# A fused Fourier mixing and shrink block: the activation's steps spread evenly over three quarters of a pass, the fourth transform step behind a product's copy, and a third PSUM bank for the transforms

## The chip, the cores and the metric

The kernel runs on one core of a Trainium2 chip, in 32-bit floating point throughout. The metric is the device time of one execution in microseconds (us); where several runs were made, their median. TensorE (PE) multiplies matrices into PSUM, which has eight banks of 2 KB for each of 128 partitions; ScalarE (ACT), VectorE (DVE) and GpSimd (POOL) do the rest, and SyncE (SP) issues most transfers. Each engine carries out its own queue in order, and semaphores tie the queues together.

## The reference

The first half mixes each sequence by a filter in the frequency domain, the second is an up projection, a shrink and a down projection:

```python
# x: (8, 3008, 256); filters: (1505, 256); w_in: (256, 2048); w_out: (2048, 256)
X = np.fft.rfft(x, axis=1)
Y = X * (filt_r + 1j * filt_i)[None]
y = np.fft.irfft(Y, n=3008, axis=1)
h = y.reshape(24064, 256) @ w_in
out = (h - np.tanh(h)) @ w_out
```

## The kernel before

**Transforms.** 3008 = 64 x 47, so a Fourier transform is cut into small matmuls. The eight batches are taken in five groups: batch 0, pairs (1,2), (3,4), (5,6), and batch 7. For each group there are four kinds of step. `first` (L351) multiplies input rows into the PSUM tile `pf`, and ScalarE copies it out. `middle` multiplies into `pz` (L430); ScalarE makes two half copies `zs` of it (L443 and L444), VectorE multiplies `pz` by the filter's real part (L445, which the program orders behind those copies), and GpSimd multiplies `zs` by the imaginary part (L446) and adds (L447), giving `uv`. `back`, one step later, multiplies `uv` into `pe` (L411), which ScalarE copies out (L414). `last` multiplies into `pu` (L511), which ScalarE copies into `ut` (L513), and GpSimd forms the four combinations `tu` (L524 to L527, a helper shared with the shrink).

**Passes.** The two projections run over 48 column groups, each of 512 tokens (fewer in the last group of a batch or pair). A group is taken in four passes (the loop variable U, 192 in all), each for a quarter of the 2048 hidden features. Both projections use a 2 x 2 Strassen-like scheme of seven products in place of eight, on halves of 256 tokens. So "product 4" is the fourth of seven, and each product is two matmuls of 128x128 by 128x256. Pass U does, interleaved: the up projection of pass U, the shrink of pass U-1, and the down projection of pass U-2. Function `up` writes this order out by hand, and calls `s()`, `d()` and `e()` for the next step of the shrink, of the down projection and of its tail, and `t(k)` for at most one transform step at "quarter" k.

**Up projection.** Seven products (all at L545) go to three PSUM banks, X, Y and Z, in the order X1, Y2, X6, Z5, X7, X4, Z3: a product adds onto what the bank holds. Copies on ScalarE (L551) keep X's state after products 1, 6 and 7 as `s1`, `u2` and `u3`; VectorE then writes the four blocks of h: Y + s1 (L569), Z + u3 (L583), X itself (L590) and Z + u2 (L596). The next product into X has to wait for the copy of X: product 7 for u2, product 4 for u3, product 1 of the next pass for L590.

**Shrink.** h - tanh(h) is approximated for small |h| by h * y * ((A y + B)^2 + K), where y is the square of arctan(S h). It works on two halves of h, called 2 (blocks 2 and 3) and 0 (blocks 0 and 1), each 128 x 1024. For each: Arctan (L611) and Square (L612, which also leaves row sums that a later check of the range reads) and a second Square (L618), all on ScalarE; a product with h (L617) and a fused add and multiply (L621) on VectorE. The text calls L617 of half 0 mul(0), and L621 of half 0 L621(0). When both halves are done GpSimd forms the combinations t for the down projection (L524 to L527).

**Down projection.** At L663, into four banks o0 to o3 that gather over the four passes of a group: products 1 and 2, then 3 and 5, then 6 and 7, then 4. In the second pass of the group after (those with U = 1 modulo 4) a tail works the sums off: L676 and L682 on ScalarE, L677, L683, L688, L689 and L695 on VectorE, L690 and L696 on GpSimd. The output's transposes (L713, VectorE) come in the pass after that, at quarter 2.

**Order in a pass on TensorE.** X1, Y2, t(0), down 1 and 2, t(1), X6, Z5, down 3 and 5, t(2), X7, down 6 and 7, t(3), X4, down 4, t(4), Z3. Which quarters hold a transform step is laid down by positions computed per batch group; in passes with U = 3 modulo 4, quarters 0 and 2 hold the two `last` steps. The eighth PSUM bank, T, and the bank of Y are what transforms use: function `zd` gives T, or at quarters 1 to 3, if the transform before had T, Y's bank. Asking for a tile in a bank makes its first writer wait for the last reader of the tile before it.

**Stages.** From about 160 to 480 us nearly every quarter holds a transform step (the dense stage); then come, for each pair of batches, a stage with `first` steps and one with `middle` and `back` steps (the latter two from 710 to 1150 us and, for the next pair, some 570 us later); then the same with the single last batch; from about 2455 us on no transforms.

Of the kernel before, what the change touches and what calls it, by code (L numbers as in the profile page):

```python
# [9 lines left out]
F32 = mybir.dt.float32  # L10
# [133 lines left out]
def kernel(  # L144
# [10 lines left out]
    V, G, ACT = nc.vector, nc.gpsimd, nc.scalar  # L155
# [367 lines left out]
    def combine(b, t, shared=False):  # L523
        G.tensor_sub(t[0], b[0][1], b[0][0])  # L524
        G.tensor_sub(t[1], b[1][1], t[0])  # L525
        (V if shared else G).tensor_sub(t[2], b[1][1], b[0][1])  # L526
        G.tensor_sub(t[3], t[1], b[1][0])  # L527
# [4 lines left out]
    def up(U, d, e, s, t):  # L532

        i, u = divmod(U, 4)
        b, tu, w = uts[i]
        rhs = [b[0][0], b[1][0], b[1][1], tu[:, 3, 0:w], tu[:, 0, 0:w], tu[:, 1, 0:w],
               tu[:, 2, 0:w]]
        banks = {k: ps.tile([128, 2, 256], F32, tag=k, bufs=1, name=k) for k in "xyz"}
        X, Y, Z = (banks[k][:, :, 0:w] for k in "xyz")
        h = dn.tile([128, 4, 2, 256], F32, tag="h", bufs=3, name="h")  # L540
        hs[U] = (h, w)

        def mm(bank, q, first):
            for k in range(2):
                nc.tensor.matmul(bank[:, k], wu[:, q - 1, (2 * u + k) * 128:(2 * u + k + 1) * 128],  # L545
                                 rhs[q - 1], start=(first and k == 0), stop=True,
                                 skip_group_check=True)

        def copied(tag):
            t = dn.tile([128, 2, 256], F32, tag=tag, bufs=1, name=tag)[:, :, 0:w]  # L550
            ACT.copy(t, X)  # L551
            return t

        steps_at = ([1, 2, 0, 1, 0, 1, 1, 0] if U > 1 else [0, 0, 1, 0, 2, 0, 1, 2])

        def shrinks(at):
            for _ in range(steps_at[at]):  # L560
                s()

        mm(X, 1, True)
        mm(Y, 2, True)
        s1 = copied("s1")
        t(0)
        d()
        shrinks(0)
        V.tensor_add(h[:, 0, :, 0:w], Y, s1)  # L569
        e()  # L570
        shrinks(1)
        t(1)
        mm(X, 6, False)
        mm(Z, 5, True)
        u2 = copied("u2")
        shrinks(2)
        d()
        shrinks(3)
        e()
        t(2)  # L580
        mm(X, 7, False)
        u3 = copied("u3")
        V.tensor_add(h[:, 3, :, 0:w], Z, u3)  # L583
        shrinks(4)
        d()
        shrinks(5)
        e()
        t(3)
        mm(X, 4, False)
        V.tensor_copy(h[:, 2, :, 0:w], X)  # L590
        shrinks(6)
        d()
        e()
        t(4)
        mm(Z, 3, False)
        V.tensor_add(h[:, 1, :, 0:w], Z, u2)  # L596
        shrinks(7)

    def shrink(U):

        h, w = hs.pop(U)
        ht = {k: h[:, k:k + 2].rearrange("p a b n -> p (a b) n")[:, :, 0:w] for k in (0, 2)}

        def tiles(tag, bufs):
            return dn.tile([128, 4, 256], F32, tag=tag, bufs=bufs, name=tag)[:, :, 0:w]

        y, sq = {}, {}

        def start(k):
            y[k] = tiles("y", 2)  # L610
            ACT.activation(y[k], ht[k], AF.Arctan, scale=S)  # L611
            ACT.activation(y[k], y[k], AF.Square,  # L612
                           accum_out=y_sums[:, 2 * U + k // 2:2 * U + k // 2 + 1])

        def square(k):
            sq[k] = tiles("sq", 1)
            V.tensor_mul(ht[k], ht[k], y[k])  # L617
            ACT.activation(sq[k], y[k], AF.Square, bias=near_b, scale=A)  # L618

        def end(k):  # L620
            V.scalar_tensor_tensor(out=ht[k], in0=sq[k], scalar=K, in1=ht[k],  # L621
                                   op0=ALU.add, op1=ALU.mult)

        start(2)
        yield
        square(2)
        yield
        end(2)
        yield
        start(0)  # L630
        yield
        square(0)
        yield
        end(0)
        t = dn.tile([128, 4, 2, 256], F32, tag="t", bufs=2, name="t")
        blocks = [[h[:, 2 * a + k, :, 0:w] for k in range(2)] for a in range(2)]
        combine(blocks, [t[:, k, :, 0:w] for k in range(4)], U + 1 == 4 * len(groups))
        gs[U] = (blocks, t, w)
        yield
# [64 lines left out]
    def store(i, o):  # L704


        p, c = groups[i]
        r, n = CHUNKS[p][c]
        ws_ = widths(p, c)
        total = sum(ws_)  # L710
        ot = dn.tile([128, 2, CH * 128], F32, tag="ot", bufs=1, name="ot")
        for h in range(2):
            V.transpose(ot[:, h, 0:total], o[:, h, 0:total])  # L713
        b = UNITS[p][0]
        if len(UNITS[p]) == 2:
            blocks = [(r + 32 * q * NR, n, 32 * q) for q in range(4)]
        else:
            blocks = [(r_h + 32 * q * NR, n_h, rows.start + 32 * q)
                      for _, rows, r_h, n_h in halves(p, r, n) for q in range(2)]
        for h in range(2):  # L720
            for k in range(4):
                for row, m, lo in blocks:
                    outs.append((
                        dram(out.tensor, (b * SEQ + row) * DM + h * 128 + 32 * k,
                             [[NR * DM, 32], [DM, m], [1, 32]]),
                        ot[32 * k:32 * k + 32, h, :].rearrange(
                            "p (j c) -> p j c", c=128)[:, 0:m, lo:lo + 32]))
# [26 lines left out]
    def store_some(n):  # L754
        for dst, src in outs[:n]:
            nc.sync.dma_start(dst, src)
        del outs[:n]
# [81 lines left out]
    with tc.tile_pool(name="tr", bufs=2) as tr, tc.manual_schedule():  # L839
        with tc.tile_pool(name="pro", bufs=1) as pro, \  # L840
                tc.tile_pool(name="ps0", bufs=6, space=bass.MemoryType.PSUM) as ps0:

            def z0(name, shape):
                return ps0.tile(shape, F32, tag="z", bufs=6, name=name)
# [132 lines left out]
            for j in range(NK // 2):  # L977
# [6 lines left out]
                pz = z0("pz", [128, 2, DM])  # L984
                for i in range(2):
                    k = (2 * j + i) % 4
# [34 lines left out]
        with tc.tile_pool(name="dn", bufs=2) as dn, \  # L1021
                tc.tile_pool(name="ps", bufs=1, space=bass.MemoryType.PSUM) as ps:

            quarter, latest = [1], ["t"]

            def zd(name, shape):
                latest[0] = "y" if quarter[0] in (1, 2, 3) and latest[0] == "t" else "t"
                return ps.tile(shape, F32, tag=latest[0], bufs=1, name=name)  # L1030

            psums.append(zd)

            y_sums = dn.tile([128, 2 * 4 * len(groups)], F32, bufs=1, name="y_sums")
# [35 lines left out]
            for U in range(total + 2):  # L1070
# [27 lines left out]
                def d():  # L1098

                    next(dw, None)  # L1100

                def e():

                    next(dw, None)

                def s():

                    next(sh, None)

                def t(k):  # L1110


                    nonlocal ms, done
                    quarter[0] = k
                    if k == 2 and stores:
                        store(*stores.pop())
                    store_some(4)
                    if U >= total:
                        return
                    pos = 20 * c + 5 * u + k  # L1120
                    if u == 3 and k in (0, 2) and i + 1 < len(groups):
                        next(lasts)
                    elif done < len(steps) and steps[done] <= pos:
                        if done < n_f:
                            next(fs)
                        else:
                            next(ms)
                        done += 1
                        if done == n_f:
                            ms = middle(p + 1, z1)  # L1130
                            next(ms)
                    next(late, None)
                    if U > 0 and k in (1, 3):
                        next(copies, None)

                if U < total:
                    if U == total - 1:
                        one = tr.tile([128, 128], F32, tag="x", bufs=3, name="one_sb")
                        nc.sync.dma_start(one, one_d)
                        ones = cst.tile([128, 1], F32, name="ones")  # L1140
                        G.memset(ones, 1.0)
                    up(U, d, e, s, t)
                else:
                    for k in range(5):
                        s()
                        s()
                        d()
                        e()
                        t(k)
                        if U == total + 1 and k == 0:  # L1150
                            bounded(z1)
# [39 lines left out]
```

## Time and profile before

| what | value |
|---|---|
| time, median of three runs | 2817.25 us (2815.60 to 2819.74) |
| span of the profiled run | 2817.1 us |
| mean granted TensorE clock | 0.991 |
| L617 on VectorE | 384 times, 1491 ns in the mean |
| L621 on VectorE | 384 times, 1478 ns |
| L611, L612, L618 on ScalarE | 384 times each, 1042, 1040, 1134 ns |
| copies s, u at L551 on ScalarE | 576 times, 570 to 577 ns |
| L446, L447 on GpSimd | 112 times each, 1505 and 1881 ns |
| L445 on VectorE | 112 times, 688 ns |
| HBM traffic | 217.53 MB, 77 GB/s over the span |

The share of an engine's busy time says how near it is to being the bound of the whole. In the list of waits, a line such as "PEld x L545 <- ACT u L551" says that TensorE's weight load for an up product stood idle until ScalarE's copy u came; then follow the sum of such idle time, how often, and the longest. In the timeline a line begins with the start and the length of an instruction; "x4" are several matmul records taken together, and square brackets hold the idle time before it and what ended it. A stretch of the run is shown as its bounds, its length, and the busy time of PE, PEld, DVE, ACT and POOL in it with the number of instructions of each, then the granted clock, the DMA share and GB/s.

### The profile page before, as it was taken

The page shows a single profiled execution, that of the slowest core. Times are in us where ns is not written, and L with a number is a line of the kernel's source. Part 1 is how long each engine was busy: PE and PEld are TensorE (multiplying, and loading weights), DVE is VectorE, ACT ScalarE, POOL GpSimd, SP SyncE. Part 2 cuts the span into 40 slices and gives each one's busy share as a digit, 9 for nine tenths or more (in the row PEclk, how much of TensorE's full clock was granted, in tenths as well). Part 3 has the DMA queues.
Part 4 walks back from the last instruction along what each step waited for, and adds up shares of the span by engine and source line. Part 5 has one row for each costly group of instructions (what it writes and reads, how often), then busy time and mean ns, then how long its engine had stood idle before and what let it go on. Part 6 is the DMA issues. An engine that isn't in the chain of part 4 may idle for free.

```text
span 2817.1 us, 36653 instructions
## 1 busy us (share of the span) xinstructions
PE 2725.6 (97%) x12438; PEld 2268.1 (81%) x12438; DVE 1913.8 (68%) x2175; ACT 1877.0 (67%) x2790; POOL 1796.2 (64%) x1407
## 2 busy tenths in 40 slices
PE   4899999999999999999999999999999999999998
PEld 2577777888878777888878887888888888898887
DVE  6755666666766676666677767666676777677776
ACT  2466776666667766666667776666666676666665
POOL 5546887544776767644576777755476666655555
PEclk7999999999999999999999999999999999999999
DMA  9854443332333322223323233112223322101010
GB/s 248 220 180 118 104 123 76 87 87 72 72 77 79 74 68 61 58 81 83 88 70 76 68 79 81 40 41 67 58 65 64 77 56 57 30 19 26 16 23 17
DMA packets 322592, 217.53 MB, mean 77 GB/s; under 512 B 224782, under 2 KB 274746, under 8 KB 322156
## 3 DMA queue, kind: packets, MB, share of 16 engines
q1 hardware_dynamic: 266826, 157.28, 24.0%
q10 hardware_dynamic: 52818, 51.53, 6.0%
q0 software_dynamic: 2752, 6.30, 0.8%
q8 instruction: 100, 1.64, 0.3%
q14 instruction: 96, 0.79, 0.1%
HBM read 138.87 MB, written 79.17 MB: 77 GB/s over the span
## 4 chain that ended last, share of the span: by engine, by line
PE 79%; ACT 8%; DVE 4%; issue 4%; DMA 3%; POOL 2%; ACTq 0%; SPq 0%; DVEq 0%; POOLq 0%
PE o L663 32%; PE x L545 20%; PE z L545 9%; PE y L545 5%; PE pe L411 3%; PE pu L511 3%; PE pz L430 3%; ACT y L611 2%; PE pf L351 2%; ACT u L551 1%; DVE h L617 1%; ACT zs L444 1%; ACT zs L443 1%; ACT y L612 1%; DVE h L590 1%
## 5 line engine op out<-in xcount | busy, mean ns | idle before, releaser
L663 PE MATMUL o<-t,wd 128*128 128x256 f32 (+2 forms) x3072 | 776.0, 375 | 1.8 <-POOL t L526 1.3
L617 DVE TENSOR_TENSOR h<-h,y 128x1024 f32<-128x1024 f32 (+2 forms) x384 | 572.4, 1491 | 275.8 <-ACT y L612 275.8
L663 PEld LDWEIGHTS o<-t,wd 128*128 128x128 f32 x3072 | 580.4, 190 | 74.1 <-POOL t L526 1.6
L545 PE MATMUL x<-tu,wu 128*128 128x256 f32 (+2 forms) x2304 | 587.6, 377 | 10.8 <-ACT u L551 10.5
L663 PE MATMUL o<-h,wd 128*128 128x256 f32 (+2 forms) x2304 | 582.3, 375 | 0.4 <-DVE h L621 0.4
L621 DVE SCALAR_TENSOR_TENSOR h<-sq,h 128x1024 f32<-128x1024 f32 (+2 forms) x384 | 567.5, 1478 | 20.6 <-ACT y L611 0.5
L524 POOL TENSOR_TENSOR t<-h 128x512 f32<-128x512 f32 (+2 forms) x192 | 240.1, 1250 | 503.7 <-DVE h L621 451.9
L545 PEld LDWEIGHTS x<-tu,wu 128*128 128x128 f32 x2304 | 426.3, 190 | 154.0 <-issue 68.9
L663 PEld LDWEIGHTS o<-h,wd 128*128 128x128 f32 x2304 | 431.1, 190 | 71.9 <-issue 18.4
L618 ACT ACTIVATE sq<-y,near_b 128x1024 f32<-128x1024 f32 (+2 forms) x384 | 435.6, 1134 | 5.0 <-DVE h L621 0.2
L611 ACT ACTIVATE y<-h 128x1024 f32<-128x1024 f32 (+2 forms) x384 | 400.0, 1042 | 15.7 <-ACT e L414 8.0
L612 ACT ACTIVATE y<-y 128x1024 f32<-128x1024 f32 (+2 forms) x384 | 399.2, 1040 | 12.2
L551 ACT COPY s<-x 128x512 f32<-128x512 f32 (+2 forms) x192 | 110.7, 577 | 441.6 <-PE x L545 433.0
L527 POOL TENSOR_TENSOR t<-t,h 128x512 f32<-128x512 f32 (+2 forms) x192 | 309.2, 1610 | 0.1
L551 ACT COPY u<-x 128x512 f32<-128x512 f32 (+2 forms) x384 | 218.9, 570 | 56.8 <-PE x L545 20.3
L525 POOL TENSOR_TENSOR t<-h,t 128x512 f32<-128x512 f32 (+2 forms) x192 | 240.8, 1254 | 15.1
L583 DVE TENSOR_TENSOR h<-z,u 128x512 f32<-128x512 f32 (+2 forms) x192 | 129.5, 674 | 176.8 <-ACT u L551 173.9
L526 POOL TENSOR_TENSOR t<-h 128x512 f32<-128x512 f32 (+2 forms) x191 | 248.0, 1298 | 0.0
L446 POOL TENSOR_TENSOR zs<-zs,ft 128x512 f32<-128x512 f32 x112 | 168.6, 1505 | 91.8 <-ACT zs L444 91.7
L447 POOL TENSOR_TENSOR uv<-uv,zs 128x512 f32<-128x512 f32 x112 | 210.7, 1881 | 15.6 <-DVE uv L445 7.2
L545 PE MATMUL x<-ut,wu 128*128 128x256 f32 (+2 forms) x768 | 198.7, 381 | 8.4 <-DVE h L590 4.8
L569 DVE TENSOR_TENSOR h<-y,s 128x512 f32<-128x512 f32 (+2 forms) x192 | 130.3, 679 | 102.0 <-PE y L545 89.1
(122 smaller groups left out, 3383.7 us busy)
## 6 DMA issues: line engine op xcount, KB each, us to landing
a<-ct SPq DMA_DIRECT2D x64, 384.0 KB, 4.0
ft<-filt SPq DMA_DIRECT2D x96, 256.0 KB, 4.7
out_dram<-ot SPq DMA_DIRECT2D x1392, 16.0 KB, 1.5
ct<-e ACTq DMA_DIRECT2D x112, 192.0 KB, 2.3
ct<-a ACTq DMA_DIRECT2D x80, 256.0 KB, 2.9
x_sb<-in_x_dram SPq DMA_DIRECT2D x69, 256.0 KB, 2.8
e<-ct SPq DMA_DIRECT2D x33, 512.0 KB, 4.5
fg<-fg SPq DMA_DIRECT2D x40, 392.0 KB, 6.2
```

What stands on the lines that cost most here:

```text
L524: G.tensor_sub(t[0], b[0][1], b[0][0])
L525: G.tensor_sub(t[1], b[1][1], t[0])
L526: (V if shared else G).tensor_sub(t[2], b[1][1], b[0][1])
L527: G.tensor_sub(t[3], t[1], b[1][0])
L545: nc.tensor.matmul(bank[:, k], wu[:, q - 1, (2 * u + k) * 128:(2 * u + k + 1) * 128], rhs[q - 1], start=(first and k == 0), stop=True, ski ...
L551: ACT.copy(t, X)
L611: ACT.activation(y[k], ht[k], AF.Arctan, scale=S)
L612: ACT.activation(y[k], y[k], AF.Square, accum_out=y_sums[:, 2 * U + k // 2:2 * U + k // 2 + 1])
L617: V.tensor_mul(ht[k], ht[k], y[k])
L618: ACT.activation(sq[k], y[k], AF.Square, bias=near_b, scale=A)
L621: V.scalar_tensor_tensor(out=ht[k], in0=sq[k], scalar=K, in1=ht[k], op0=ALU.add, op1=ALU.mult)
L663: nc.tensor.matmul(product(q), wd[:, q - 1, (2 * u + k) * 128: (2 * u + k + 1) * 128], rhs[q - 1][:, k], start=(u == 0 and k == 0 and q == ...
```

## The change

There are three edits. First, the shrink's six steps are cut anew and called at other places of the pass: step 1 is Arctan and Square of half 2, step 2 its product with h, step 3 its second Square and the Arctan of half 0, step 4 L621 of half 2, step 5 both Squares of half 0 and its product with h, step 6 L621 of half 0 and the combinations. Before, ScalarE had three activations ahead of u2, two between u2 and u3, and one behind u3; now it has two, two and two. Second, `t(3)` stands behind product 4 and its copy L590, not in front of them. Third, `zd` may give Z's bank to a transform at quarter 0, unless it is `pz`, when the one before had T; to make that possible Z's tile is asked for only just before product 5. It is meant to free TensorE of waits for copies of X, and to keep two neighbouring transforms out of one bank.

```diff
--- before.py
+++ after.py
@@ -535,8 +535,11 @@
         b, tu, w = uts[i]
         rhs = [b[0][0], b[1][0], b[1][1], tu[:, 3, 0:w], tu[:, 0, 0:w], tu[:, 1, 0:w],
                tu[:, 2, 0:w]]
-        banks = {k: ps.tile([128, 2, 256], F32, tag=k, bufs=1, name=k) for k in "xyz"}
-        X, Y, Z = (banks[k][:, :, 0:w] for k in "xyz")
+
+        def bank(k):
+            return ps.tile([128, 2, 256], F32, tag=k, bufs=1, name=k)[:, :, 0:w]
+
+        X, Y = bank("x"), bank("y")
         h = dn.tile([128, 4, 2, 256], F32, tag="h", bufs=3, name="h")
         hs[U] = (h, w)
 
@@ -554,7 +557,7 @@
 
 
 
-        steps_at = ([1, 2, 0, 1, 0, 1, 1, 0] if U > 1 else [0, 0, 1, 0, 2, 0, 1, 2])
+        steps_at = ([1, 1, 1, 1, 0, 1, 1, 0] if U > 1 else [0, 0, 1, 0, 2, 0, 2, 1])
 
         def shrinks(at):
             for _ in range(steps_at[at]):
@@ -571,6 +574,7 @@
         shrinks(1)
         t(1)
         mm(X, 6, False)
+        Z = bank("z")
         mm(Z, 5, True)
         u2 = copied("u2")
         shrinks(2)
@@ -585,9 +589,9 @@
         d()
         shrinks(5)
         e()
-        t(3)
         mm(X, 4, False)
         V.tensor_copy(h[:, 2, :, 0:w], X)
+        t(3)
         shrinks(6)
         d()
         e()
@@ -606,29 +610,38 @@
 
         y, sq = {}, {}
 
-        def start(k):
+        def turn(k):
             y[k] = tiles("y", 2)
             ACT.activation(y[k], ht[k], AF.Arctan, scale=S)
+
+        def power(k):
             ACT.activation(y[k], y[k], AF.Square,
                            accum_out=y_sums[:, 2 * U + k // 2:2 * U + k // 2 + 1])
 
+        def times(k):
+            V.tensor_mul(ht[k], ht[k], y[k])
+
         def square(k):
             sq[k] = tiles("sq", 1)
-            V.tensor_mul(ht[k], ht[k], y[k])
             ACT.activation(sq[k], y[k], AF.Square, bias=near_b, scale=A)
 
         def end(k):
             V.scalar_tensor_tensor(out=ht[k], in0=sq[k], scalar=K, in1=ht[k],
                                    op0=ALU.add, op1=ALU.mult)
 
-        start(2)
+
+        turn(2)
+        power(2)
+        yield
+        times(2)
         yield
         square(2)
+        turn(0)
         yield
         end(2)
         yield
-        start(0)
-        yield
+        power(0)
+        times(0)
         square(0)
         yield
         end(0)
@@ -1023,10 +1036,12 @@
 
 
 
             quarter, latest = [1], ["t"]
 
             def zd(name, shape):
-                latest[0] = "y" if quarter[0] in (1, 2, 3) and latest[0] == "t" else "t"
+                other = "tyyyt"[quarter[0]] if quarter[0] or name == "pz" else "z"
+                latest[0] = other if latest[0] == "t" else "t"
                 return ps.tile(shape, F32, tag=latest[0], bufs=1, name=name)
 
             psums.append(zd)
```

## The prediction

> **What bounds the kernel now.** I read the busy shares first, then the chain of waits, then TensorE's waits by releaser, then stretches of the run by stage, then the timeline.
>
> ```profile
> PE 2725.6 (97%) x12438; PEld 2268.1 (81%) x12438; DVE 1913.8 (68%) x2175; ACT 1877.0 (67%) x2790; POOL 1796.2 (64%) x1407
> ...
> PE 79%; ACT 8%; DVE 4%; issue 4%; DMA 3%; POOL 2%; ACTq 0%; SPq 0%; DVEq 0%; POOLq 0%
> ```
> TensorE is the bound; no other engine is over 68%. The change leaves the number and shape of the matmuls alone, so it can only win or lose TensorE's gaps.
>
> ```profile
> PEld x L545 <- ACT u L551: 34.5, 73, 1.9
> ...
> PEld x L545 <- DVE h L590: 24.1, 49, 2.2
> ...
> PE x L545 <- ACT u L551: 10.5, 26, 1.1
> ```
> These (sum in us, number, longest) name the two waits the change aims at: products X7 and X4 on the copies u2 and u3, and X1 on L590. A weight load's wait can overlap earlier matmuls, so 34.5 is not a loss.
>
> ```profile
> 2455.00:2780.00 325.00, 324.46 (x1612) 292.39 (x1612) 240.74 (x266) 218.13 (x323) 187.60 (x146) 1.00 0.11 21
> ```
> From 2455 us on there is no transform, and PE (first number after the stretch) is busy 324.46 of 325. Nothing is to be had there. Elsewhere I take the matmul starts from the timeline: two matmul records of 128x256 start 0.216 us apart, so an up product (4 records) is due 0.86 us after its start, and a pair of down products (8) 1.73. A later start of the next product is a loss. A pass without transforms is 12.09 us. In passes 3 to 190 the losses sum to about 58 us:
> X4 after u3 13.9 (28 times), X7 after u2 5.4 (22), X1 after L590 15.9 (45), `pe` at quarter 1 after Y's reader 10.9 (8), the rest single places. Passes 0 to 2 lose 8.5.
>
> **What the Trainium skill says.** "SBUF — State Buffer", section Who interferes with whom: VectorE and GpSimd share a port under an exclusive lock, and a VectorE instruction with two SBUF inputs is wholly blocked while a GpSimd one that reads SBUF holds it. The trace agrees:
>
> ```profile
> 288.16 1.28 POOL L446 TENSOR_TENSOR zs<-zs,ft 128x512 f32<-128x512 f32 x1
> 289.07 1.45 DVE L617 TENSOR_TENSOR h<-h,y 128x1024 f32<-128x1024 f32 x1
> 289.52 2.13 POOL L447 TENSOR_TENSOR uv<-uv,zs 128x512 f32<-128x512 f32 x1
> ```
> L617 (columns: start, length) ends at 290.52, which is L446's end, 289.44, plus 1.08; L447 in turn ends 1.13 after L617. So who asks second runs from the other's end.
> "PSUM — Partial Sum Buffer", section PSUM bank collisions raise a hardware error: guard by bank, not address. Here the program does so: a transform product in Z's bank must wait for L596, the last reader of the pass before.
>
> **Part 1, the steps on ScalarE.** Before u2's copy the pass had Arctan 1.04, Square 1.04 and L618 1.13 (means of L611, L612, L618); L618 moves behind u2. So ScalarE reaches u2 1.13 earlier; between u2 and u3 stood Arctan and Square (2.1), now L618 and Arctan (2.2), so it reaches u3 some 1.05 earlier. The longest lateness I find at X7 or X4 is 1.0; all of 13.9 + 5.4 = 19 goes. X4 gives up 0.86 of slack where part 2 takes a product from in front of it; no such place loses by it in my list. Behind u3 now come Square(0) and L618, and mul(0) on VectorE waits for the former's row sums (1.18 from an L612's start to its L617, at 2621.47). In the pass shown further down u3 begins at 2614.71; Square(0) would begin at 2615.20, where L618 now does, and mul(0) at 2616.38, not 2615.94: 0.44 later.
>
> **Part 2, t(3) behind X4.** With `pz` at quarter 3, L445 stands ahead of L590 on VectorE's queue and waits for two ScalarE copies of a product that itself comes first:
>
> ```profile
> 762.59 0.58 ACT L551 COPY u<-x 128x512 f32<-128x512 f32 x1 [0.22 <-PE x L545]
> ...
> 764.12 1.02 PE L430 MATMUL pz<-a,fg 94*128 94x512 f32 x2
> 764.98 1.03 PE L545 MATMUL x<-tu,wu 128*128 128x256 f32 x4
> 765.24 0.59 ACT L443 ACTIVATE zs<-pz 64x512 f32<-64x512 f32 x1 [1.01 <-PE pz L430]
> 765.85 0.58 ACT L444 COPY zs<-pz 64x512 f32<-64x512 f32 x1
> 766.46 0.69 DVE L445 TENSOR_TENSOR uv<-pz,ft 128x512 f32<-128x512 f32 x1 [1.07 <-ACT zs L444]
> 766.50 1.27 POOL L446 TENSOR_TENSOR zs<-zs,ft 128x512 f32<-128x512 f32 x1 [2.19 <-ACT zs L444]
> ...
> 767.06 0.68 DVE L590 COPY h<-x 128x512 f32<-128x512 f32 x1
> 767.66 1.22 DVE L621 SCALAR_TENSOR_TENSOR h<-sq,h 128x1024 f32<-128x1024 f32 x1
> 767.80 1.13 PE L545 MATMUL x<-ut,wu 128*128 128x256 f32 x4
> ...
> 768.79 0.68 DVE L596 TENSOR_TENSOR h<-z,u 128x512 f32<-128x512 f32 x1
> 769.63 1.05 PE L511 MATMUL pu<-s_sb,e 128*128 128x128 f32 x8
> ```
> X1 of the next pass (767.80) is due at 767.44 and waits for L590: 0.36 lost, though X4 ended at 766.0. In the new order L590 runs at about 765.1. Over all such places 12 of the 15.9 us go; the rest are passes with `pz` at quarter 4 or narrow ones.
>
> **Part 3, Z's bank at quarter 0.** The gain: a product no longer reuses the bank of the one just before it. `pe` at quarter 4 of two passes 1.1, passes 21 and 132 together 1.8, the start (0 to 2) 1.5. The sum of gains: 19 + 12 + 1.1 + 1.8 + 1.5 = 35 us.
>
> The price: after a `pz` at quarter 3 (which took T), the product at quarter 0 gets Z and waits for L596. In the example, with X4 at 764.12 and `pz` at 764.98, the copies end at 767.29, L446 runs 767.36 to 768.63, L445 to 768.0. L621 asks at 768.0 while L446 holds the port, so it runs 768.63 to 769.72; L596 behind it to 770.33. `pu` would be due at 769.29 and starts at 770.39: 1.1, and 0.1 for the semaphore and the loads. Before, the same product waited for nothing late. The two pair stages have 14 such crossings; in 4 of them the down tail's additions stand in the queue as well, 1.55: 10 x 1.2 + 4 x 1.55 = 18 us. After a `pz` at quarter 4, L445 alone (0.69) is ahead of L596: 0.35 each at 11 places, 4 us.
>
> **What else is queued behind the moved waits.**
> - L621(0) blocked by L446 also makes t late for the products 1 and 2 of the down transform: 0.53 at 6 places without a product at quarter 0, 3 us.
> - In passes 1 of 4, the tail's L688 and L689 stand between mul(0) and L590:
>
> ```profile
> 2614.71 0.58 ACT L551 COPY u<-x 128x512 f32<-128x512 f32 x1
> 2615.20 1.16 ACT L618 ACTIVATE sq<-y,near_b 128x1024 f32<-128x1024 f32 x1
> 2615.94 1.22 DVE L617 TENSOR_TENSOR h<-h,y 128x1024 f32<-128x1024 f32 x1
> 2617.86 0.68 DVE L590 COPY h<-x 128x512 f32<-128x512 f32 x1
> 2618.83 1.03 PE L545 MATMUL x<-ut,wu 128*128 128x256 f32 x4
> ```
> L590 ends at 2618.54 and X1 starts at 2618.83, as due; the slack I find is 0.05 after the semaphore and load, so mul(0) 0.44 later, some of it made up in front of L688, costs about 0.3 at some 12 such passes without a product late in the pass: 4 us.
> - mul(0) later by 0.44 comes second to POOL's L447 in passes with `pz` at quarter 2, and is blocked up to 1.1: 0.8 to 0.9 at 6 places, 5 us with small ones.
> The sum of losses: 18 + 4 + 3 + 4 + 5 = 34 us.
>
> **Left alone.** `pe` at quarter 1 keeps its bank and its 10 us. The program's end has the same order on ScalarE. In the stretch without transforms the new order of ScalarE hides behind TensorE apart from the tail passes above.
>
> **Sum.** 2817.25 - 35 + 34, with rounding about 2816.5 us. By stage: the two pair stages (710 to 1150 us and their like) 2 us slower each, the stage of single first-transform products 4 faster, the start 1.5 faster, the end 1 slower.
>
> **The rivals.**
> - Faster. Gains as above, but the Z waits come to half, since a loss at quarter 0 gives the other engines 1.2 us that later waits then don't cost, and since L621 may ask before L446 takes the port (a margin of 0.6 in the example). The Z and mul(0) terms at half: 34 falls to 22, hence about 2805. For it: my losses are summed place by place, and two in one pass are not both paid in full. Against it: L445 and L446 are released by the same copy, so L446 starts first whenever L445 does.
> - Slower. The gains are partly moved waits: X4 freed of u3 meets the next bound, and L596 late by 1.2 delays h1 and so the next pass's Arctan. With 26 of the 35 gained and the losses a little over (36): 2827. For it: ScalarE is 67% busy and gets 2.3 us of work behind u3, where the copies of `pz` also queue. Against it: the chain X1, u2, u3 is shorter by a full L618.
> - All gains and no Z waits, 2799: only if a product in Z were released early. The program's order of waits speaks against it.
>
> **How the numbers follow.** The forecast, balance, 0.44; its error from some 60 small terms is 5 us either way, so 0.32 within 0.2% (5.6 us), 0.08 below, 0.04 above. The faster rival with its extreme 0.32 (0.30 below, 0.02 within). The slower one 0.24 (0.21 above, 0.03 within). Together 0.38, 0.37, 0.25. Range 2803 to 2829: it takes in both middle rivals with 2 us beyond, and leaves out the extreme.
>
> **What would show it.** Right: X4 and X7 no longer released by u (34.5 falls to a few us); X1 after L590 falls to near 4 us; new lines in which `pu` and `pe` wait for L596, in 25 places, longest about 1.5; L621 of the pass stretched past 1.6 us after a `pz` at quarter 3; L617 of pass 2 of 4 near 2.3. Wrong: `pu` after `pz` at quarter 3 not waiting (then faster), or new waits of X7, X4 or of the down products on L621 beyond 5 us (then slower).

## The result and the profile after

The changed kernel takes 2839.2 us (median of six, 2836.45 to 2842.18) against 2817.76: the ratio is 1.0076, 95% interval 1.0063 to 1.0089. That is 21.4 us slower, outside the range of the prediction and not the balance that it forecast. The profiled run has a span of 2838.3 us, 21.2 more than before.

The page of the changed kernel, busy time by engine and the chain that ended last:

```profile
PE 2723.3 (96%) x12438; PEld 2270.5 (80%) x12438; DVE 1897.2 (67%) x2175; ACT 1886.8 (66%) x2790; POOL 1748.1 (62%) x1407
...
PE 81%; DVE 7%; ACT 6%; DMA 2%; issue 2%; POOL 1%; ACTq 0%; SPq 0%; DVEq 0%; POOLq 0%
```

TensorE does the same work in the same time (2723 us against 2726), so the 21 us are gaps. In the chain VectorE's share rose from 4 to 7% and ScalarE's fell from 8 to 6%: a first sign of which engine now holds TensorE up. Line numbers have shifted: L548 is the up product, L554 the copies s and u, L572 the first block of h, L593 the copy of X (L590 before), L600 the add that reads Z (L596 before), L629 the fused add and multiply (L621 before), L676 the down product.

TensorE's waits after the change (sum in us, number, longest):

```profile
PEld x L548 <- DVE h L593: 19.9, 33, 1.3
...
PE pe L411 <- DVE h L600: 11.7, 14, 1.3
PEld pe L411 <- DVE h L600: 11.2, 8, 1.6
...
PEld pu L511 <- DVE h L600: 8.7, 11, 1.3
...
PE pe L411 <- DVE uv L445: 8.2, 6, 1.4
...
PEld x L548 <- ACT u L554: 4.1, 5, 2.3
```

The weight loads' waits for u have gone from 34.5 us to 4.1, as the change meant. The waits for L600 are the forecast ones, with about the forecast length (longest 1.6 us, 1.5 forecast). The wait for L445 in the fifth line was not in the prediction: six times pe waits for the reader of another product.

By stage, with the stretches set at the starts of the same passes. First the kernel before, then the changed one (bounds, length, busy PE, PEld, DVE, ACT and POOL with counts, granted clock, DMA share, GB/s):

```profile
258.50:480.80 222.30, 214.71 (x894) 162.94 (x893) 140.16 (x158) 160.11 (x244) 182.72 (x129) 1.00 0.43 106
...
709.80:1138.40 428.60, 424.00 (x1875) 342.48 (x1875) 294.97 (x314) 299.88 (x444) 312.59 (x226) 1.00 0.31 72
...
2454.70:2779.00 324.30, 323.76 (x1610) 291.69 (x1608) 239.88 (x265) 218.13 (x323) 187.90 (x146) 1.00 0.10 21
```
```profile
263.10:495.00 231.90, 215.82 (x894) 162.58 (x893) 141.28 (x159) 160.34 (x244) 172.67 (x129) 1.00 0.40 101
...
724.20:1154.60 430.40, 421.68 (x1875) 343.07 (x1875) 292.46 (x314) 300.77 (x444) 302.34 (x225) 1.00 0.31 72
...
2472.20:2798.10 325.90, 324.82 (x1610) 290.73 (x1608) 238.54 (x265) 220.16 (x323) 188.24 (x146) 1.00 0.10 20
```

The first line of each is the dense stage (passes 9 to 21): 9.6 us longer, with the same 894 matmul records, where the prediction by stage had no change. The second is the first pair stage, 1.8 longer (2 was forecast; its twin, which begins at 1385.9 us before and so 676 us later, not some 570, is 2.0 longer); the third has no transforms, 1.6 longer (the end was forecast 1 slower). The starts of the passes give the rest of the span: 4.6 up to pass 9, nothing in the stages of first-transform steps (together -0.7), 0.2 in the last batch's `middle` and `back` stage, and 2.1 after the start of pass 191.

**A forecast wait, seen.** The crossing from pass 42 to 43 in the timeline of the changed kernel:

```profile
778.68 1.02 PE L430 MATMUL pz<-a,fg 94*128 94x512 f32 x2
...
779.39 0.68 DVE L593 COPY h<-x 128x512 f32<-128x512 f32 x1
...
781.02 0.69 DVE L445 TENSOR_TENSOR uv<-pz,ft 128x512 f32<-128x512 f32 x1 [0.95 <-ACT zs L444]
...
781.06 1.27 POOL L446 TENSOR_TENSOR zs<-zs,ft 128x512 f32<-128x512 f32 x1 [2.68 <-ACT zs L444]
781.27 1.03 PE L548 MATMUL x<-ut,wu 128*128 128x256 f32 x4
781.63 1.79 DVE L629 SCALAR_TENSOR_TENSOR h<-sq,h 128x1024 f32<-128x1024 f32 x1
...
782.13 1.03 PE L548 MATMUL y<-ut,wu 128*128 128x256 f32 x4
...
783.34 0.68 DVE L600 TENSOR_TENSOR h<-z,u 128x512 f32<-128x512 f32 x1
...
784.07 1.16 PE L511 MATMUL pu<-s_sb,e 128*128 128x128 f32 x8 [0.91 <-DVE h L600]
```

L593 now runs right behind product 4, and X1 (781.27) is on time. But L629 is asked for while L446 has the port: its length is 1.79 us, and it ends at 783.42, which is L446's end (782.33) plus 1.09. L600 follows at 783.34, and `pu`, due 0.86 us after Y2 at 782.99, starts at 784.07: 1.08 lost; the prediction had 1.1.

**The wait that was not forecast.** Pass 9, in the dense stage of the changed kernel:

```profile
275.58 1.03 PE L548 MATMUL x<-tu,wu 128*128 128x256 f32 x4
...
276.44 1.02 PE L430 MATMUL pz<-a,fg 94*128 94x512 f32 x2
...
277.30 1.03 PE L676 MATMUL o<-t,wd 128*128 128x256 f32 x4
...
278.90 0.68 DVE L445 TENSOR_TENSOR uv<-pz,ft 128x512 f32<-128x512 f32 x1
...
279.73 1.07 PE L411 MATMUL pe<-uv,fg 112*96 112x512 f32 x2 [1.40 <-DVE uv L445]
```

`pe` at quarter 4 is due at 278.16 and starts at 279.73, once L445 has read the `pz` of quarter 3: both have bank T. Quarter 0 took Z in this pass, so quarter 1 got T, quarter 2 Y, quarter 3 T, and at quarter 4 the rule `"tyyyt"[4]` knows only T. Before, the same five products went T, Y, T, Y, T. The same place in the kernel before:

```profile
270.59 1.02 PE L430 MATMUL pz<-a,fg 94*128 94x512 f32 x2
...
273.38 1.02 PE L411 MATMUL pe<-uv,fg 112*96 112x512 f32 x2
...
274.06 0.68 DVE L445 TENSOR_TENSOR uv<-pz,ft 128x512 f32<-128x512 f32 x1
```

Here `pe` starts before L445 has read `pz`. One more bank at the front of the row has turned the order by one, and the two products at its end, which part 2 has also brought nearer to each other, share a bank.

### The profile page after: what moved, and what is told of

It reads as the page before. It is cut to its first block, busy times and chain, and to the rows that moved or that the text cites. A ratio compares the mean times of both kernels' runs of the same rounds, so it can differ in the third digit from the quotient of the medians.

```text
span 2838.3 us, 36481 instructions
## 1 busy us (share of the span) xinstructions
PE 2723.3 (96%) x12438; PEld 2270.5 (80%) x12438; DVE 1897.2 (67%) x2175; ACT 1886.8 (66%) x2790; POOL 1748.1 (62%) x1407
## 3 DMA queue, kind: packets, MB, share of 16 engines
q1 hardware_dynamic: 266826, 157.28, 23.9%
## 4 chain that ended last, share of the span: by engine, by line
PE 81%; DVE 7%; ACT 6%; DMA 2%; issue 2%; POOL 1%; ACTq 0%; SPq 0%; DVEq 0%; POOLq 0%
PE o L676 35%; PE x L548 20%; PE z L548 9%; PE y L548 5%; PE pe L411 3%; PE pz L430 3%; PE pu L511 3%; PE pf L351 2%; DVE h L622 1%; ACT y L618 1%; DVE h L629 1%; ACT zs L443 1%; ACT zs L444 1%; DVE uv L445 1%; DMA raw<-in_moe_w_in_dram 1%
## 5 line engine op out<-in xcount | busy, mean ns | idle before, releaser
L676 PE MATMUL o<-t,wd 128*128 128x256 f32 (+2 forms) x3072 | 777.0, 375 | 1.8 <-POOL t L526 1.3
L676 PEld LDWEIGHTS o<-t,wd 128*128 128x128 f32 x3072 | 580.6, 190 | 101.6 <-issue 30.4
L629 DVE SCALAR_TENSOR_TENSOR h<-sq,h 128x1024 f32<-128x1024 f32 (+2 forms) x384 | 549.7, 1432 | 122.9 <-ACT sq L626 114.3
L676 PE MATMUL o<-h,wd 128*128 128x256 f32 (+2 forms) x2304 | 583.6, 376 | 4.0 <-DVE h L629 4.0
L548 PE MATMUL x<-tu,wu 128*128 128x256 f32 (+2 forms) x2304 | 583.1, 375 | 3.3 <-ACT u L554 3.1
L524 POOL TENSOR_TENSOR t<-h 128x512 f32<-128x512 f32 (+2 forms) x192 | 240.2, 1251 | 555.7 <-DVE h L629 405.9
L548 PEld LDWEIGHTS x<-tu,wu 128*128 128x128 f32 x2304 | 430.9, 190 | 105.0 <-issue 43.5
L676 PEld LDWEIGHTS o<-h,wd 128*128 128x128 f32 x2304 | 431.3, 190 | 77.8 <-issue 19.6
L554 ACT COPY s<-x 128x512 f32<-128x512 f32 (+2 forms) x192 | 110.8, 577 | 323.7 <-PE x L548 299.5
L554 ACT COPY u<-x 128x512 f32<-128x512 f32 (+2 forms) x384 | 220.7, 575 | 139.9 <-PE x L548 125.7
L525 POOL TENSOR_TENSOR t<-h,t 128x512 f32<-128x512 f32 (+2 forms) x192 | 247.5, 1289 | 15.1
L446 POOL TENSOR_TENSOR zs<-zs,ft 128x512 f32<-128x512 f32 x112 | 163.9, 1463 | 131.6 <-ACT zs L444 131.3
L526 POOL TENSOR_TENSOR t<-h 128x512 f32<-128x512 f32 (+2 forms) x191 | 241.5, 1264 | 0.0
L447 POOL TENSOR_TENSOR uv<-uv,zs 128x512 f32<-128x512 f32 x112 | 203.4, 1816 | 8.8
L548 PE MATMUL x<-ut,wu 128*128 128x256 f32 (+2 forms) x768 | 197.3, 379 | 8.4 <-DVE h L593 6.8
L548 PE MATMUL z<-tu,wu 128*128 128x256 f32 (+2 forms) x768 | 194.1, 375 | 0.6 <-ACT a L352 0.6
```

The costliest lines, as they stand in the source:

```text
L676: nc.tensor.matmul(product(q), wd[:, q - 1, (2 * u + k) * 128: (2 * u + k + 1) * 128], rhs[q - 1][:, k], start=(u == 0 and k == 0 and q == ...
```

## The experiments

Each was timed beside the kernel before, whose median was 2817.4 to 2818.3 us. By the intervals (the changed kernel's is 1.0063 to 1.0089) a difference between two rows is good to some 3 to 5 us.

| kernel | us | ratio to before, 95% interval |
|---|---|---|
| changed, old bank rule (no_z) | 2812.3 | 0.9979 (0.9973 to 0.9986) |
| before with part 1 (only_steps) | 2817.9 | 0.9998 (0.9989 to 1.0007) |
| before with part 2 (only_move) | 2825.2 | 1.0026 (1.0018 to 1.0033) |
| before with part 3 (only_z) | 2830.3 | 1.0045 (1.0030 to 1.0061) |
| changed, other bank for pe at quarter 4 (parity_q4) | 2830.1 | 1.0041 (1.0027 to 1.0055) |
| changed, t(3) after the sixth step (t3_last) | 2845.3 | 1.0100 (1.0085 to 1.0116) |
| no_z, t(3) after the sixth step (no_z_t3_last) | 2843.5 | 1.0087 (1.0074 to 1.0101) |
| changed, Z not after pz (z_not_after_pz) | 2811.4 | 0.9974 (0.9966 to 0.9983) |
| z_not_after_pz, first block of h at once (h0_first) | 2802.2 | 0.9943 (0.9930 to 0.9956) |
| z_not_after_pz, mul(0) late in tail passes (tail_late) | 2811.2 | 0.9975 (0.9968 to 0.9981) |
| the last two together | 2803.4 | 0.9945 (0.9931 to 0.9958) |

I also summed TensorE's late starts after 162 us, put down to the instruction that ended the wait, as the prediction did (us; the columns leave out waits for uv, the end of the run and single places). Six kernels are in the table, figures of the others in the text:

| kernel | X after u | X1 after its copy | pu, pe after the add on Z | pe after L445 | pe at quarter 1 after L569/L572 | down 1, 2 after L621/L629 | all |
|---|---|---|---|---|---|---|---|
| before | 19.3 | 16.0 | 0 | 1.1 | 7.5 | 0.7 | 68.6 |
| changed | 1.4 | 15.9 | 22.2 | 9.2 | 7.7 | 4.4 | 87.1 |
| no_z | 1.6 | 18.8 | 0 | 2.9 | 7.4 | 4.3 | 57.6 |
| only_steps | 0.7 | 30.9 | 0 | 1.5 | 7.4 | 0.9 | 66.6 |
| only_move | 27.1 | 7.6 | 0 | 2.9 | 7.4 | 4.1 | 71.2 |
| only_z | 18.8 | 15.5 | 7.2 | 6.5 | 7.7 | 0.7 | 76.4 |

**The three parts, one taken out and each alone.**

```diff
 # no_z: the changed kernel with
-                other = "tyyyt"[quarter[0]] if quarter[0] or name == "pz" else "z"
-                latest[0] = other if latest[0] == "t" else "t"
+                latest[0] = "y" if quarter[0] in (1, 2, 3) and latest[0] == "t" else "t"
```

> The changed kernel with the bank rule of the kernel before (part 3 undone, parts 1 and 2 kept). Theory A, Z's bank is the harm: the 22 us of waits for L600 (the add that reads Z) go, and so do the 9.4 us in which pe at quarter 4 waits for L445 in the dense stage, since pz at quarter 3 is back in another bank; some 3 us that the third bank saved come back (passes 21, 67, 115, 132). About 2811 us, faster than before. Theory B, the later work on ScalarE is the harm (mul(0) and L629 late, so the down products and X1 wait): at most the pe and pu lines change and the time stays above 2825.

2812.3 us: theory A, to 1.3 us. Z's bank costs 27 us on top of the other two parts, and without it they are 5.4 us faster than the kernel before. Theory B is out as the main harm: the later work on ScalarE stays in this kernel. It does cost something here, as 18.8 us at X1 against 16.0 before and 4.3 at the down products against 0.7 show.

```diff
 # only_steps: no_z with
-        mm(X, 4, False)
-        V.tensor_copy(h[:, 2, :, 0:w], X)
         t(3)
+        mm(X, 4, False)
+        V.tensor_copy(h[:, 2, :, 0:w], X)
```

> The kernel before with part 1 alone, the re-cut steps. Theory A: X4 and X7 waits for u fall by 18 us; mul(0) later costs some 3.5 us in the passes with the tail, 5 us behind GpSimd's L447, 2 to 4 us at the start and 2 at the end: about 2810 us. Theory B: slower than before, 2820 or more, with the losses at X1 after L590 and at the down products.

2817.9, no change: a miss for both theories, though the losses are at X1, where B had put them. Its waits (L594 is here the copy of X):

```profile
PEld x L548 <- DVE h L594: 40.2, 66, 1.3
...
PE x L548 <- DVE h L594: 13.7, 40, 0.9
...
PEld x L548 <- ACT u L554: 3.0, 4, 1.9
```

The waits for u are gone, 18.6 us of lateness, and 14.9 come back at X1 after its copy. Part of it is the later mul(0), which the passes with the tail and the narrow groups pay; in passes with `pz` at quarter 3 the old wait of the copy behind L445 is still there, since this kernel has the old place of t(3). The gain of part 1 alone is moved, not won.

```diff
 # only_move: the kernel before with
-        t(3)
         mm(X, 4, False)
         V.tensor_copy(h[:, 2, :, 0:w], X)
+        t(3)
```

> The kernel before with part 2 alone, t(3) behind product 4. Theory A: X1 after L590 loses 10 to 12 us of its 15.9; product 4 comes 0.86 earlier where quarter 3 has a transform and so waits for u3 in more places, 4 to 6 us more; 3 us at down products 1 and 2 after L621(0). About 2813 us. Theory B, the move itself makes the products at quarters 3 and 4 collide: pe at quarter 4 waits in the dense stage though banks alternate, 9 us, and the time is 2820 or more.

2825.2, slower; a miss. Both sides of theory A show, in other sizes (L551 are here the copies u, L589 the copy of X):

```profile
PEld x L545 <- ACT u L551: 42.1, 80, 2.2
...
PE x L545 <- ACT u L551: 16.2, 31, 1.8
...
PEld x L545 <- DVE h L589: 11.9, 22, 2.1
```

X1 wins 8.4 us and X4 and X7 lose 7.8 more to u3 and u2, because product 4 now comes 0.86 us sooner. In the table 3.4 us more are at down products 1 and 2. Theory B, that products of quarters 3 and 4 collide by the move itself, fails: pe after L445 is 2.9, not 9. The profiled run lost only 3.6 us against before where the median lost 7.5; the start of a run differs by several us from one to the next (pass 9 begins between 255 and 266 us in these profiles), so I count parts by the waits and not by spans. The median's other 4 us are not in this profile, and stay open.

The three together say that parts 1 and 2 need each other: part 1 alone 0.1, part 2 alone 7.5, both -5.4 us. Part 1 takes the waits for u that part 2 makes (27.1 to 1.6), and part 2 takes L445 from in front of the copy (X1 30.9 to 18.8).

```diff
 # only_z: the kernel before with the bank rule and the late Z tile of the changed one
```

> The kernel before with part 3 alone, Z's bank at quarter 0. Theory A, the collisions need part 2's later pz: pu and pe after pz at quarter 3 find L596 done (no loss), 4 us after pz at quarter 4, and pe at quarter 4 in the dense stage waits 0.7 in 6 places, 4 us; gains 3 us. About 2822 us. Theory B, Z's bank alone is the whole harm: 30 us of waits, 2845 us.

2830.3 us, between the two theories (2822 and 2845). The waits are of A's kinds, 7.2 after the add on Z (4 forecast) and 5.4 more after L445 (4), 7.8 us more lateness in all; the median is 12.6 longer, and the rest I can't place from one profile.

**Which banks collide.**

```diff
 # parity_q4: the changed kernel with
...
+                if name == "pe" and quarter[0] == 4 and last_q[0] == 3:
+                    other = "y"
+                last_q[0] = quarter[0]
                 latest[0] = other if latest[0] == "t" else "t"
```

> The changed kernel, but a pe at quarter 4 right behind a product at quarter 3 that has T takes Y's bank. Theory A (after Z at quarter 0 the banks' order is turned by one, so that pz at quarter 3 and pe at quarter 4 both get T and pe waits for L445): the six waits of 1.5 to 1.6 us in the dense stage go, 9 us, the waits for L600 stay: about 2830 us. Theory B (pe at quarter 4 is late because t(3) behind product 4 has crowded ScalarE and VectorE there): the waits move to another line and the time stays at 2837 or more.

2830.1: theory A. No wait of pe for L445 is left (9.2 before the edit), all others are as they were, and 9.1 us are won. The six collisions of the dense stage come from the bank order; only_z, without part 2, has 6.5 of the 9.2 us already.

**Why the add on Z is late.**

```diff
 # t3_last: the changed kernel with
-        t(3)
         shrinks(6)
+        t(3)
```

> The changed kernel with t(3) called after the shrink's sixth step, so that L629(0) and the combinations come ahead of L445 and L446 on VectorE and GpSimd; TensorE's order is the same. Theory A (L600 is late because L629(0) ahead of it is shut out by L446): the waits of pu and pe for L600 after a pz at quarter 3 fall from 1.1 to 1.5 us to under 0.4, 14 us together, and the down products' waits for L629, 3.4 us, go too: about 2822 us. Theory B (L600 is late because of L445 and the sheer number of adds): the waits stay, 2836 or more. In either, pe may wait for the later uv.

2845.3: the time is a miss, the mechanism is theory A's. The same crossing in its timeline:

```profile
787.47 1.21 DVE L629 SCALAR_TENSOR_TENSOR h<-sq,h 128x1024 f32<-128x1024 f32 x1
...
788.60 0.68 DVE L445 TENSOR_TENSOR uv<-pz,ft 128x512 f32<-128x512 f32 x1
...
788.83 1.27 POOL L524 TENSOR_TENSOR t<-h 128x512 f32<-128x512 f32 x1 [2.96 <-DVE h L629]
789.20 0.68 DVE L600 TENSOR_TENSOR h<-z,u 128x512 f32<-128x512 f32 x1
```

L629 takes 1.21 us, not 1.79, and L600 runs 0.45 us after X1's start (788.75), where it ran 2.07 after it (783.34 against 781.27). The waits after the add on Z fall from 22.2 to 7.4 us, 14.8 for 14 forecast, and those of the down products from 4.4 to 0.9. But L446 now stands behind the four combinations on GpSimd, of 1.25 us or more each, uv comes later by that, and pe waits for it:

```profile
PEld pe L411 <- POOL uv L447: 20.8, 8, 4.8
...
PE pe L411 <- POOL uv L447: 14.5, 5, 4.4
...
PE pe L411 <- DVE uv L445: 11.6, 6, 2.5
```

```diff
 # no_z_t3_last: no_z with the same move
```

> Without Z's bank, and t(3) after the shrink's sixth step. L629(0) is not shut out by L446 any more: down products 1 and 2 win 4 us: 2808 us. Against it: L446 and L447 come behind the four combinations on GpSimd, some 5 us later, and a pe that wants that uv soon waits; then 2815 or more.

2843.5: the objection holds, and costs far more than the 4 us at stake (of those 3.4 are won, 4.3 to 0.9). pe after uv is 37.1 us, up from 5.5, most of it in the dense stage, where the next quarter wants the uv.

**Z's bank only where it is free.**

```diff
 # z_not_after_pz: the changed kernel with
...
-                other = "tyyyt"[quarter[0]] if quarter[0] or name == "pz" else "z"
+                other = "tyyyt"[quarter[0]]
+                if quarter[0] == 0 and "pz" not in (name, before[0]):
+                    other = "z"
+                before[0] = name
```

> The changed kernel, with Z's bank at quarter 0 only where the transform before was not pz. The L600 waits of the pair and dense stages go with the bank order that they turn; the gains of Z's bank in the first-transform stages stay (2 us). Theory A: 2810 us, as without Z's bank or a little less. Theory B (Z's bank costs elsewhere, too): 2818 or more.

2811.4: theory A. Against no_z it is 0.9 us, within the intervals, so Z's bank at quarter 0 has no clear gain of its own here.

**What was left.** Two of the waits that the changed kernel keeps were tried on top of this.

```diff
 # h0_first
         s1 = copied("s1")
+        V.tensor_add(h[:, 0, :, 0:w], Y, s1)
         t(0)
         d()
         shrinks(0)
-        V.tensor_add(h[:, 0, :, 0:w], Y, s1)
```

> Z's bank only where the transform before was not pz, and the first block of h (L572, which reads Y's bank) taken right after s1, ahead of t(0) and so of L445 on VectorE. Theory: pe at quarter 1 in Y's bank waits in the dense stage only because L572 stands behind L445, which waits for the zs copies; then the 7.4 us of waits for L572 go and nothing comes in their place: about 2804 us. Rival: the wait turns into one for ScalarE's copies or for uv: 2810 or more.

2802.2: 9.2 us from 2811.4, and the theory's 7.4 within the error of such a difference. First the wait in the changed kernel (pass 10), then the same place in this one:

```profile
285.62 0.69 DVE L445 TENSOR_TENSOR uv<-pz,ft 128x512 f32<-128x512 f32 x1 [3.22 <-ACT zs L444]
...
286.23 0.68 DVE L572 TENSOR_TENSOR h<-y,s 128x512 f32<-128x512 f32 x1
...
287.05 1.07 PE L411 MATMUL pe<-uv,fg 112*96 112x512 f32 x2 [1.07 <-DVE h L572]
```
```profile
281.55 0.68 DVE L569 TENSOR_TENSOR h<-y,s 128x512 f32<-128x512 f32 x1
...
283.52 0.69 DVE L445 TENSOR_TENSOR uv<-pz,ft 128x512 f32<-128x512 f32 x1 [1.30 <-ACT zs L444]
283.72 1.02 PE L411 MATMUL pe<-uv,fg 112*96 112x512 f32 x2
```

L445 waits for ScalarE either way; the add in front of it (L569 in this kernel) costs nothing and frees Y's bank 2.6 us earlier, counted from Y2's start (282.37 and 280.27). This kernel beats both: 0.9943 of the time before.

```diff
 # tail_late: in passes 1 of 4 with no transform due at quarter 3
...
+        after_copy[U - 1] = u == 1 and not due(3)
         shrinks(5)
...
 # and in the shrink's steps 5 and 6
-        times(0)
+        if not after_copy.get(U, False):
+            times(0)
         square(0)
         yield
+        if after_copy.get(U, False):
+            times(0)
         end(0)
```

> Z's bank only where the transform before was not pz, and mul(0) after L590 in the passes with the tail's additions that have no transform at quarter 3. Theory (mul(0), later by 0.44 behind the row sums, pushes L590 and so X1 of the next pass): about 0.33 at each of some 12 to 15 passes comes back, 4 to 5 us: 2807 us. Rival: L621(0), now later by 0.7, makes down products 1 and 2 wait instead: no change, 2811.

2811.2, the rival. Its waits (L596 is here the copy of X, L632 the fused add and multiply, L682 the down product):

```profile
PEld x L550 <- DVE h L596: 19.3, 31, 1.2
...
PEld o L682 <- DVE h L632: 14.8, 37, 2.6
```

Without the edit they were 23.9 in 41 places and 10.8 in 23: X1's late starts fell from 18.7 to 15.2, while those of the down products rose from 4.6 to 6.1 and single places took the rest. VectorE has that much to do between product 4 and the next down products, and this edit of its order only chose who waits.

> Both of these edits together. If they are independent their gains add: about 2800 us.

2803.4, within the intervals of 2802.2: the one gain, and nothing from the other.

## Why the prediction was wrong, by its steps

- Part 1 (X4 and X7, 19 us): right, 19.3 to 1.4. Part 3's price after `pz` (18 + 4): right, 22.2, and t3_last shows the cause to be the one given, L621 (now L629) shut out by L446. The down products (0.7 to 4.4, 3 forecast) and the pair stages (1.8 and 2.0, 2 each) were right as well.
- The first step that failed is Part 3, whose price counted only the product that takes Z's bank. It said that the gain is a product which "no longer reuses the bank of the one just before it". The order of the banks behind it was taken as unchanged, so six collisions of `pe` with `pz` at quarters 3 and 4 were missed: pe after L445 went from 1.1 to 9.2 us, where part 3 had the 1.1 as a gain. parity_q4 takes these away and wins 9.1 us. That is the largest single term of a miss of some 22 us, and less than half of it.
- The second is the balance of parts 1 and 2. With its own terms the prediction has them 19 us faster together (31 gained; 3, 4 and 5 lost); no_z, which has these two alone, is 5.4 faster. The largest term of this is X1: Part 2's "12 of the 15.9 us go", with 4 + 5 us coming back, made X1 3 us better, and in no_z it is 2.8 worse (18.8; 15.9 in the changed kernel). (The sign "falls to near 4 us" left out the 9 us that its own sum puts back.) The gain was had (12.1 from only_steps to no_z, 8.4 from before to only_move), but part 1 puts 14.9 on in the one order (only_steps) and 11.2 in the other (only_move to no_z), not 9: in the changed kernel's trace they are at the tail passes and behind L447, as listed, and at narrow groups (passes 71, 119, 122, 167), which were not. In no_z pe after L445 is 1.8 more, X4 and X7 give 1.3 less and the down products cost 0.6 more than forecast; some 4 us of the 13.6 that are short I can't place.
- The start, forecast 1.5 faster: pass 3 begins 2.2 us later than before, and in pass 2 the first down products wait 2.0 us for L629. Pass 8 waits 4.3 us for uv, against 3.0 before; in both kernels the granted clock is at half for 3.4 us after it. But passes up to 9 vary by several us between runs of the same code or nearly so, so which part of this is the change stays open.
- The stage of single first-transform products, forecast 4 faster, is 0.9 faster (242.2 to 241.3): new waits at X1 there, the same mul(0).
- The end, forecast 1 slower with its last waits as before, is 1.6 slower up to pass 191 and 2.1 more behind its start. There the granted clock was 0.66 in a stretch of 5 us (2816 to 2821), behind a wait of 1.46 us that the kernel before has too, without the loss of clock; so I don't lay this to the change.
- Of the 10.9 us of `pe` at quarter 1 that were left alone, 3.0 are a wait for uv in pass 8 and only 7.5 one for Y's reader; h0_first shows that the 7.5 could be had with one moved line.

Of the rivals, the slower one named the right side and a part of the cause: X4 freed of u3 does meet the next bound, X1 after its copy (14.9 us more in only_steps, 11.2 from only_move to no_z). The bank order it did not have, and 2827 was still too low.

## What to carry to other kernels

When a buffer is added to a rotation, write down the new owner of every buffer down the whole row, not only at the place where it is added: a rule that picks "the other one" by position shifts all that follows. Two edits of which one gives nothing and the other loses can win together, when each takes away the wait that the other one opens, so test an edit's parts both out of the whole and alone. Look for a read that frees a shared bank behind an instruction that waits for another engine: here moving one such read ahead won 9.2 us.

## What the runs showed of the hardware

A wait of TensorE can cost more than itself. In no_z_t3_last pe starts at 286.06, 4.4 us late, and the next dozen records are 0.43 us apart instead of 0.216, so some 3 us go on top. The windows of that kernel show the granted clock (third number from the end) under half way and back:

```profile
284.00:290.00 6.00, 3.94 (x7) 2.42 (x8) 0.89 (x1) 0.75 (x2) 5.17 (x4) 0.61 0.41 103
290.00:296.00 6.00, 6.00 (x22) 4.72 (x21) 2.65 (x4) 3.80 (x6) 0.17 (x1) 0.82 0.13 28
296.00:302.00 6.00, 6.00 (x25) 4.46 (x25) 5.04 (x6) 4.31 (x7) 3.03 (x3) 1.00 0.41 80
```

The four waits of 4.4 us up to 440 us (246, 286, 362 and 439 us) all did this; of three of about 2.5 us (324, 400 and 476 us) the last two did and the first did not. The Trainium skill ("TensorE: Matmul & The Clock Gate", section What's actually happening) has the clock at half rate by default and after an idle window of about 3.4 us, free-running. The waits of 4.4 us fit; those of 2.5 us are shorter than such a window, so here one that was idle only in part was enough. The halved clock can account for what no_z_t3_last and t3_last lose beyond their waits. Between 162 us and pass 191 the granted clock is at half for 41 us in no_z_t3_last and 3.4 in no_z, which at half rate is at most some 19 us more lost; late starts at single places, put down to none of the waits named here, rise from 10.1 us in no_z to 27.3. From the changed kernel to t3_last it is 3.4 to 27 us at half, and 14.8 to 24.7 us late.
